# Partition shuffles with another stride and another issuing engine in a convolution-plus-MLP kernel

## The chip, the cores and the metric

The kernel runs on one core of one Trainium2 chip. Times are device microseconds (us) of one launch. The time before the change is 325.86 us, the median of two runs (324.25 and 327.46).

A core has five engines that take their instructions in order: PE (matmul), ACT (scalar engine), DVE (vector engine), POOL (GpSimd) and SP, which only issues here. Copies between memories go through 16 DMA engines. SP, ACT and POOL can each issue such transfers, on queues of their own.

## What is computed

```python
def _A_ref(q, k, v, shift_k, ssm_k, ssm_D):      # q, k, v: 1 x 2048 x 448
    k_shift = ...                                # causal convolution of k with 4 taps
    kv = k_shift * v
    y = irfft(rfft(kv, 4096) * rfft(ssm_k, 4096))[:2048]   # long convolution
    y = y + kv * ssm_D
    return q * y

def _B_ref(x, w1, b1, w2, b2):
    h = layernorm(x)
    u = gelu(einsum("bsd,sf->bdf", h, w1) + b1)  # f = 1792
    y = einsum("bdf,fs->bds", u, w2) + b2
    return y.transpose(0, 2, 1)

h  = x + _A_ref(layernorm(x), k, v, shift_k, ssm_k, ssm_D)
h2 = h + _B_ref(layernorm(h), w1, b1, w2, b2)    # x = q; layernorm over the 448 channels
```

The calls to the FFT are shortened here; the FFT runs along the sequence, each of the 448 channels on its own, and the sequence of 2048 is padded to 4096. All inputs and the output are bf16.

## The kernel before, in words

**Layout.** A sequence position is written as 16 q + r, with q on the 128 partitions and r = 0..15 along the partition. So each input is a tile of 128 x 16 x 448. All tiles lie at fixed offsets of one SBUF tensor, `arena`; PSUM is one tensor `ps` of eight banks, each 128 x 512 floats.

**The FFT as two stages of matmuls with a shuffle between.** Stage 1 (`emit_stage1`, L828) takes each r in turn: two matmuls (L832 with the cosine table `Ct`, L834 with the sine table `St`), which give 128 frequencies x 448 channels, real and imaginary, in a pair of PSUM banks; one evacuation (L839, on ACT or DVE) into one of eight ring buffers `WR`, 128 partitions x 1,792 bytes; then a *shuffle*, a DMA (L841) from that ring buffer into the tile T. The shuffle reads all 128 partitions and writes eight: source partition 16 i + j becomes row j of destination partition r + 16 i (`T[r:128:R]`, R = 16). After the 16 shuffles T holds, for row j, all 16 values of r on the partitions, and stage 2 (`emit_stage2`, L848) runs per row j four matmuls (L854) with 128 x 128 tables that mix the 16 partitions of one group, and one evacuation (L621/L622 on ACT, L624/L625 on DVE, all through the helper `evac`) in place. This is done for the filter `ssm_k` (tile TK, tag "k") and for kv (tile TU, tag "u").

**Products and inverse transform.** `emit_products_i1` (L872) multiplies the two spectra row by row (L877, L882 on DVE), runs eight matmuls per row (L888), evacuates, and sends the row through a third set of 16 shuffles (L893, `TZ[j:128:R]`) into TZ. `emit_i2` (L943) is the last stage: per r three matmuls into one bank (L951 adds kv times D, L953 and L955 use the transposed tables `CTt`, `STt` made by PE transposes in `emit_ct`, L864), then the product with the normalised q (L958), the residual (L961) and the statistics for the second layernorm (L964, L967, L971 to L983; the power -0.5 runs on POOL, L975 and L978). The first layernorm, of q, is `emit_q` (L914 to L927, its power on POOL, L919 and L922). `emit_kvd` (L935) multiplies kv by D.

**MLP.** L1017 and L1025 multiply by w1 (14 chunks of 128), L1008 is the gelu, L1034 multiplies by w2, L1037 adds, L1041 and L1044 store. The weights lie in memory that earlier tiles leave free and are loaded from ACT's queue: L996 (first part of w1, two transfers of 1,536 KB), L999 (the rest), L1004 (w2, four transfers). The first w2 transfer overwrites rows of TU that the third set of shuffles reads.

**The tables.** `emit_tables` (L630) makes `Ct` and `St` and the four block tables CC, NCC, SS, NSS (cosine and sine, with both signs) with iotas on POOL, integer and mask work on DVE (L671 to L724) and sines on ACT. The same four block tables serve stage 2 and the inverse transform.

**What sets the order.** All operations are first collected with what they read and write, then a list scheduler (`_Sched.schedule`, L236) gives each to an engine at a time of its own model and so fixes the order of every engine's instructions. It takes the ready operation with the longest remaining path first. Its costs are constants: issuing a DMA costs 450 ns on SP or ACT and 1,100 on POOL; a transfer uses `keng` DMA engines (8 for a shuffle) at 22 bytes per ns each. Buffers in rings (PSUM banks, the eight `WR`) are acquired at the moment of issue in the model: an operation that writes a pair takes any two free banks. Waits are then emitted from the true dependencies, on semaphores.

Of the kernel before, what the change touches and what calls it, by code (L numbers as in the profile page):

```python
# [71 lines left out]
class _Pool:  # L72
    def __init__(self, n):
        self.n = n
        self.free_t = [0.0] * n
        self.prev = [[] for _ in range(n)]
# [21 lines left out]
class _Sched:  # L98
# [137 lines left out]
    def schedule(self):  # L236
# [41 lines left out]
        def can_acquire(o):  # L278
            need = {}
            for b in o.acq:  # L280
                need[b.pool] = need.get(b.pool, 0) + b.k
            for p, k in need.items():
                if sum(1 for x in p.free_t if x <= t + 1e-6) < k:
# [195 lines left out]
def _build(nc, A_q, A_k, A_v, A_shift_k, A_ssm_k, A_ssm_D, B_w1, B_b1, B_w2, B_b2, out):  # L479
# [52 lines left out]
    o_SM = o_CC + 4 * 256  # L532
    SMALL = o_SM
    NSMALL = 3328

    ctx = ExitStack()
    with ctx:
# [43 lines left out]
        CC = view(o_CC, [128], f16)  # L581
        NCC = view(o_CC + 256, [128], f16)
        SS = view(o_CC + 512, [128], f16)
        NSS = view(o_CC + 768, [128], f16)
# [15 lines left out]
        psum = _Pool(8)  # L600
# [6 lines left out]
        def Ppair(b):  # L607
            s0, s1 = b.slots
            return PS[:, s0:s1 + 1:s1 - s0, 0:D]
# [4 lines left out]
        FX = ("act", "dve")  # L614

# [14 lines left out]
        def emit_tables():  # L630
# [6 lines left out]
            o_p = small(16)  # L637
# [3 lines left out]
            pc = view(o_p, [4], i32)  # L641
            pcf = view(o_p + 8, [2], f32)
# [3 lines left out]
            o_dv = o_TT + 4 * (HALF + 128)  # L646
            o_sv = o_dv + 4 * (HALF + 128)
            pi_ = view(o_pi, [HALF + 128], i32)
            dv_ = view(o_dv, [HALF + 128], f32)
            ssm = view(o_sv, [128], f32)  # L650
            csm = view(o_sv + 512, [128], f32)
            msk = view(o_sv + 1024, [128], f32)
            chi = view(o_sv + 1536, [128], i32)
            idi = view(o_sv + 2048, [128], i32)
# [9 lines left out]
            op("pool", lambda e, W: e.iota(idi, [[1, 128]], base=0, channel_multiplier=-1), w=[(o_sv + 2048, 512)],  # L664
# [5 lines left out]
               w=[(o_sv + 1536, 512)], n=128, kind="iota")  # L670
            op("dve", lambda e, W: e.tensor_single_scalar(out=ID, in_=idi, scalar=0.0, op=ALU.is_equal),  # L671
               r=[(o_sv + 2048, 512)], w=[(o_ID, 256)], n=128)
            op("dve", lambda e, W: e.tensor_copy(out=IH, in_=ID), r=[(o_ID, 256)], w=[(o_IH, 256)], n=128)
            op("dve", lambda e, W: e.tensor_scalar(out=pc[:, 1:2], in0=pc[:, 0:1], scalar1=15, scalar2=None,
                                                   op0=ALU.bitwise_and), r=[(o_p, 4)], w=[(o_p + 4, 4)], n=1)
            op("dve", lambda e, W: e.tensor_copy(out=pcf[:, 0:1], in_=pc[:, 1:2]), r=[(o_p + 4, 4)],
               w=[(o_p + 8, 4)], n=1)
            op("dve", lambda e, W: e.tensor_scalar(out=pc[:, 1:2], in0=pc[:, 0:1], scalar1=4, scalar2=None,
                                                   op0=ALU.logical_shift_right), r=[(o_p, 4)], w=[(o_p + 4, 4)], n=1)
            op("dve", lambda e, W: e.tensor_copy(out=pcf[:, 1:2], in_=pc[:, 1:2]), r=[(o_p + 4, 4)],  # L680
               w=[(o_p + 12, 4)], n=1)
            for h in range(2):
                n = HALF if h == 0 else HALF + 128
# [6 lines left out]
                if h == 1:  # L690
                    op("dve", lambda e, W: e.tensor_scalar(out=pi_[:, HALF:HALF + 128], in0=cmod,
                                                           scalar1=pcf[:, 0:1], scalar2=None, op0=ALU.mult),
                       r=[(o_cm, 512), (o_p + 8, 4)], w=[(o_pi + 4 * HALF, 512)], n=128)
# [406 lines left out]
```

## Time and profile before

The profile is one execution. "Busy" is the time in which an engine ran instructions; times in the trace count from the start of the span.

| | |
|---|---|
| median of the runs shown | 325.86 us |
| the profiled execution | 326.04 us |
| its span, first to last instruction | 324.2 us |
| busy: PE, DVE, ACT, POOL | 66%, 37%, 34%, 6% |
| mean granted clock of PE | 0.783 of full speed |
| moved by DMA | 35.95 MB, 111 GB/s over the span |
| bytes in the 48 shuffles | 48 x 224 KB = 11.0 MB |
| stages by time, us | loads and filter transposes to 23; stage 1 and shuffles 23 to 105 (stage 2 of k inside); stage 2 of u 105 to 147; products and inverse 147 to 202; last shuffle to 214; last stage and statistics to 229; MLP 229 to 324 |

How to read the rows in the next part. A row of the *chain* has its start, its length and what it was: the chain is followed back from the last instruction to whatever released it. A row of *busy time by stretch* has the stretch, its length, then for PE, PE's weight loads, DVE, ACT and POOL the busy time (and the count), then the granted PE clock, the mean busy share of the 16 DMA engines and the GB/s moved. A row of the *timeline* has start, length, engine, line, operation, what is written and read, and in brackets the idle time before it with what ended that. SPq and ACTq are the queues' issues. A row of *waits* has who waited for whom, total us, times, longest. A row of *one line's instructions* has shortest, median and longest ns, and the first and last start.

### The profile page before, as it was taken

The page shows a single profiled execution, that of the slowest core. Times are in us where ns is not written, and L with a number is a line of the kernel's source. Part 1 is how long each engine was busy: PE and PEld are TensorE (multiplying, and loading weights), DVE is VectorE, ACT ScalarE, POOL GpSimd, SP SyncE. Part 2 cuts the span into 40 slices and gives each one's busy share as a digit, 9 for nine tenths or more (in the row PEclk, how much of TensorE's full clock was granted, in tenths as well). Part 3 has the DMA queues.
Part 4 walks back from the last instruction along what each step waited for, and adds up shares of the span by engine and source line. Part 5 has one row for each costly group of instructions (what it writes and reads, how often), then busy time and mean ns, then how long its engine had stood idle before and what let it go on. Part 6 is the DMA issues. An engine that isn't in the chain of part 4 may idle for free.

```text
span 324.2 us, 2484 instructions
## 1 busy us (share of the span) xinstructions
PE 213.5 (66%) x913; PEld 96.8 (30%) x913; DVE 121.5 (37%) x241; ACT 110.0 (34%) x168; POOL 18.3 (6%) x45
## 2 busy tenths in 40 slices
PE   0656434474960766667766446065799999999994
PEld 0511000011330211112222112022354445667772
DVE  8499980006670597001244400049730000003034
ACT  6597434453440333332233223026970122210000
POOL 1000000001020024000000000000530000000000
PEclk9978555559795665555599959559599999999999
DMA  7996555555996000001229579629500000000022
GB/s 199 294 433 176 108 108 111 110 110 114 163 204 175 14 0 0 0 0 27 53 66 259 140 232 271 171 49 381 232 1 0 2 0 0 2 0 28 30 85 86
DMA packets 16279, 35.95 MB, mean 111 GB/s; under 512 B 1100, under 2 KB 10572, under 8 KB 16139
## 3 DMA queue, kind: packets, MB, share of 16 engines
q1 hardware_dynamic: 10250, 21.11, 25.3%
q10 hardware_dynamic: 6016, 14.68, 16.0%
q8 instruction: 7, 0.11, 0.1%
q14 instruction: 6, 0.04, 0.1%
HBM read 22.94 MB, written 1.84 MB: 76 GB/s over the span
## 4 chain that ended last, share of the span: by engine, by line
PE 47%; DMA 31%; ACT 13%; DVE 5%; issue 1%; SPq 1%; DVEq 0%; ACTq 0%
DMA arena<-arena 28%; PE ps L1034 13%; ACT arena L621 10%; PE ps L888 10%; PE ps L854 8%; PE ps L1025 8%; PE ps L1017 6%; DMA arena<-in_A_ssm_k_dram 3%; ACT arena L839 3%; DVE arena L958 2%; DVE arena L961 1%; PE ps L817 1%; DVE arena L1037 1%; SPq L743 0%; DVE arena L624 0%
## 5 line engine op out<-in xcount | busy, mean ns | idle before, releaser
L854 PE MATMUL ps<-arena 128*128 128x448 bf16 x128 | 43.0, 491 | 31.1 <-ACT arena L621 13.6
L621 ACT CAST arena<-ps 128x896 bf16<-128x896 f32 (+1 forms) x32 | 28.2, 881 | 78.7 <-PE ps L854 38.0
L888 PE MATMUL ps<-arena 128*128 128x448 bf16 x128 | 34.4, 424 | 20.8 <-ACT arena L621 20.8
L1034 PE MATMUL ps<-arena 128*128 128x448 bf16 x224 | 45.6, 355 | 0.0
L1037 DVE SCALAR_TENSOR_TENSOR arena<-ps,arena 128x448 bf16<-128x448 f32 x16 | 9.7, 677 | 69.0 <-PE ps L1034 69.0
L839 ACT CAST arena<-ps 128x896 bf16<-128x896 f32 x29 | 25.6, 931 | 29.4 <-DMA arena<-arena 26.2
L1034 PEld LDWEIGHTS ps<-arena 128*128 128x128 bf16 x224 | 31.5, 145 | 13.5 <-ACT arena L1008 3.1
L832 PE MATMUL ps<-arena 128*128 128x448 bf16 x32 | 16.0, 501 | 25.7 <-ACT arena L839 19.9
L854 PEld LDWEIGHTS ps<-arena 128*128 128x128 f16 x128 | 13.2, 119 | 59.8 <-ACT arena L621 23.8
L1025 PE MATMUL ps<-arena 128*128 128x448 bf16 x128 | 29.4, 353 | 0.0
L1017 PE MATMUL ps<-arena 128*128 128x448 bf16 x96 | 23.7, 386 | 5.8 <-DVE arena L983 5.8
L877 DVE TENSOR_TENSOR arena<-arena 128x896 bf16<-128x896 bf16 x16 | 10.0, 625 | 43.5 <-PE ps L888 42.6
L888 PEld LDWEIGHTS ps<-arena 128*128 128x128 f16 x128 | 12.9, 111 | 42.6 <-ACT arena L621 29.9
L1008 ACT ACTIVATE arena<-ps,arena 128x448 bf16<-128x448 f32 x14 | 8.9, 633 | 40.4 <-PE ps L1017 21.1
L958 DVE TENSOR_TENSOR arena<-ps,arena 128x448 bf16<-128x448 f32 x16 | 9.4, 623 | 29.7 <-PE ps L955 29.6
L798 DVE TENSOR_TENSOR arena<-arena 128x1792 bf16<-128x1792 bf16 x16 | 16.5, 1098 | 4.0 <-DMA arena<-in_A_k_dram 4.0
L832 PEld LDWEIGHTS ps<-arena 128*128 128x128 f16 x32 | 3.3, 102 | 46.7 <-ACT arena L839 38.5
L834 PE MATMUL ps<-arena 128*128 128x448 bf16 x32 | 16.5, 516 | 0.0
L1025 PEld LDWEIGHTS ps<-arena 128*128 128x128 bf16 x128 | 12.0, 98 | 12.6 <-ACT arena L1008 2.4
L964 ACT ACTIVATE arena<-arena 128x448 bf16<-128x448 bf16 x16 | 9.2, 576 | 17.3 <-PE ps L953 16.9
L1017 PEld LDWEIGHTS ps<-arena 128*128 128x128 bf16 x96 | 10.1, 106 | 16.3 <-DVE arena L983 6.3
L953 PE MATMUL ps<-arena 128*128 128x448 bf16 x16 | 6.8, 425 | 11.2 <-DMA arena<-arena 11.2
(74 smaller groups left out, 184.4 us busy)
## 6 DMA issues: line engine op xcount, KB each, us to landing
arena<-arena SPq DMA_DIRECT2D x48, 224.0 KB
arena<-in_B_w_dram ACTq DMA_DIRECT2D x5, 2048.0 KB, 9.9
arena<-in_B_w_dram ACTq DMA_DIRECT2D x2, 1536.0 KB, 25.6
arena<-in_A_ssm_k_dram SPq DMA_DIRECT2D x4, 448.0 KB, 7.8
arena<-in_A_k_dram SPq DMA_DIRECT2D x4, 448.0 KB, 12.4
arena<-in_A_v_dram SPq DMA_DIRECT2D x4, 448.0 KB, 13.0
arena<-in_A_q_dram SPq DMA_DIRECT2D x1, 1792.0 KB, 19.0
out_dram<-arena SPq DMA_DIRECT2D x7, 224.0 KB, 1.9
```

The costliest lines, as they stand in the source:

```text
L621: return e.copy(out=dst(), in_=src())
L798: op("dve", lambda e, W, T=T, i=i, r=r: e.tensor_tensor(out=T[:, i], in0=KH[:, r:r + 4, :], in1=WT, op=ALU.mult), r=[(o_KH + r * DB, 4 * D ...
L832: op("pe", lambda e, W, b=b, r=r: e.matmul(Pb(b, 0), Ct[:, r, :], src[:, r, :], start=True, stop=True), r=[r_C(r), (o_src + r * DB, DB)], ...
L834: op("pe", lambda e, W, b=b, r=r: e.matmul(Pb(b, 1), St[:, r, :], src[:, r, :], start=True, stop=True), r=[r_S(r), (o_src + r * DB, DB)], ...
L839: return e.copy(out=dst, in_=Ppair(b)) if W == "act" else e.tensor_copy(out=dst, in_=Ppair(b))
L854: op("pe", lambda e, W, b=b, bi=bi, tab=tab, ci=ci, st=st, sp=sp, j=j: e.matmul(Pb(b, bi), tab, T[:, j, ci, :], start=st, stop=sp), r=rr, ...
L888: i = op("pe", lambda e, W, b=b, bi=bi, tab=tab, mi=mi, m=m, k=k: e.matmul(Pb(b, bi), tab, MR(m.slots[0])[:, mi, :], start=(k % 4 == 0), s ...
L958: op("dve", lambda e, W, b=b, r=r: e.tensor_tensor(out=V[:, r, :], in0=Pb(b), in1=Q[:, r, :], op=ALU.mult), r=[(o_Q + r * DB, DB)], w=[(o_ ...
L1017: op("pe", lambda e, W, r=r, fc=fc, b=bs[fc]: e.matmul(Pb(b), W1A[:, r, 128 * fc:128 * fc + 128], Q[:, r, :], start=(r == 0), stop=(r == R ...
L1025: op("pe", lambda e, W, r=r, fc=fc, b=b: e.matmul(Pb(b), W1B[:, r, 128 * (fc - n0):128 * (fc - n0) + 128], Q[:, r, :], start=(r == 0), sto ...
L1034: op("pe", lambda e, W, r=r, fc=fc, b=b: e.matmul(Pb(b), W2[:, fc, r:S:R], G[:, fc, :], start=(fc == 0), stop=(fc == NFC - 1)), r=[(o_W2 + ...
L1037: op("dve", lambda e, W, r=r, b=b: e.scalar_tensor_tensor(out=X[:, r, :], in0=Pb(b), scalar=b2c[:, r:r + 1], in1=X[:, r, :], op0=ALU.add, ...
```

## The change

**Stride and issuer.** Shuffle r now writes the eight partitions p0, p0 + 4, ..., p0 + 28 with p0 = 32 (r >> 2) + (r & 3), in place of r, r + 16, ..., r + 112. All three sets of shuffles are issued from POOL (`SHQ`), where descriptors are written by software, in place of SP.

**What follows from it.** Partition 32 a + 4 i + b now holds frequency group i and value r = 4 a + b. Stage 2 therefore gets block tables of its own (FC, FS, FNS) beside the four that the inverse transform keeps, so there are seven. For the last stage, the tables are reordered before they are transposed: four copies of 128 x 1,024 elements on POOL (`emit_ct`).

**PSUM pairs.** A pair of banks is now an aligned pair (0 and 1, 2 and 3, ...), and a single bank is taken by preference where the other half of its pair is in use. The evacuation reads two adjacent banks.

```diff
 class _Pool:
-    def __init__(self, n):
+    def __init__(self, n, pairs=False):
...
+        def pick(p, k):
+
+            ok = [x <= t + 1e-6 for x in p.free_t]
+            if k == 1:
+                best = None
+                for i in range(p.n):
+                    if ok[i]:
+                        key = (p.pairs and ok[i ^ 1], p.free_t[i], i)
+                        if best is None or key < best:
+                            best = key
+                return None if best is None else [best[2]]
+            best = None
+            for i in range(0, p.n, 2):
+                if ok[i] and ok[i + 1]:
+                    key = (max(p.free_t[i], p.free_t[i + 1]), i)
+                    if best is None or key < best:
+                        best = key
+            return None if best is None else [best[1], best[1] + 1]
...
-                        fr = sorted((x, i) for i, x in enumerate(p.free_t) if x <= t + 1e-6)[:b.k]
-                        b.slots = sorted(i for _, i in fr)
+                        b.slots = pick(p, b.k)
...
-        psum = _Pool(8)
+        psum = _Pool(8, pairs=True)
...
+        SHQ = ("pool", "pool")
...
-                n = HALF if h == 0 else HALF + 128
+                n = HALF if h == 0 else HALF + 256
...
+            for k, (so, sgn, i) in enumerate(((1, 1.0, 0), (0, 1.0, 0), (0, -1.0, 0), (1, 1.0, 1), (1, -1.0, 1),
+                                              (0, 1.0, 1), (0, -1.0, 1))):
+                src = (ssm, csm)[so][:, 128 * i:128 * i + 128]
+                op("dve", lambda e, W, k=k, src=src, sgn=sgn, i=i: e.scalar_tensor_tensor(
+                    out=BD[k], in0=src, scalar=sgn, in1=msk[:, 128 * i:128 * i + 128], op0=ALU.mult, op1=ALU.mult),
...
-                op("sp", lambda e, W, w=w, r=r: e.dma_start(T[r:128:R].rearrange("p j c d -> p j (c d)"),
-                                                            WR(w.slots[0]).rearrange("p c d -> p (c d)")),
+                p0 = 32 * (r >> 2) + (r & 3)
+                op(SHQ[r % 2], lambda e, W, w=w, p0=p0: e.dma_start(
+                    T[p0:p0 + 29:4].rearrange("p j c d -> p j (c d)"),
+                    WR(w.slots[0]).rearrange("p c d -> p (c d)")),
...
-                for bi, tab, ci, st, sp in ((0, CC, 0, True, False), (0, NSS, 1, False, True),
-                                            (1, SS, 0, True, False), (1, CC, 1, False, True)):
+                for bi, tab, ci, st, sp in ((0, FC, 0, True, False), (0, FNS, 1, False, True),
+                                            (1, FS, 0, True, False), (1, FC, 1, False, True)):
...
         def emit_ct():
...
+                    op("pool", lambda e, W, cp=cp, tab=tab, h=h: e.tensor_copy(
+                        out=cp.rearrange("p r (h f l) -> p r h f l", h=4, f=8),
+                        in_=tab[:, 8 * h:8 * h + 8, :].rearrange("p r (f h l) -> p r h f l", f=8, h=4)),
+                       r=[(o_tab + 2048 * h, 2048)], w=[(oc, 2048)], n=1024)
...
-                op("sp", lambda e, W, j=j: e.dma_start(TZ[j:128:R].rearrange("p r c d -> p r (c d)"),
-                                                       TU[:, j].rearrange("p c d -> p (c d)")),
+                p0 = 32 * (j >> 2) + (j & 3)
+                op(SHQ[j % 2], lambda e, W, j=j, p0=p0: e.dma_start(
+                    TZ[p0:p0 + 29:4].rearrange("p r c d -> p r (c d)"), TU[:, j].rearrange("p c d -> p (c d)")),
```

More of the change, by code (lines that the diff above doesn't have):

```diff
@@ L72 @@
 class _Pool:
-    def __init__(self, n):
+    def __init__(self, n, pairs=False):
         self.n = n
+        self.pairs = pairs
         self.free_t = [0.0] * n
@@ L282, in can_acquire @@
             for p, k in need.items():
-                if sum(1 for x in p.free_t if x <= t + 1e-6) < k:
+                if pick(p, k) is None:
                     return False
             return True
+        def pick(p, k):
[15 more added lines that the diff above has]
+            return None if best is None else [best[1], best[1] + 1]
         while done < n:
@@ L580, in _build @@
         IH = view(o_IH, [128], f16)
[L581 to L584, printed above, removed]
+        BD = [view(o_CC + 256 * k, [128], f16) for k in range(7)]
+        FC, FS, FNS, CC, NCC, SS, NSS = BD
         def WR(s):
@@ L640, in emit_tables @@
             srow = view(o_s, [16], i32)
[L641 to L642 removed]
+            pc = view(o_p, [6], i32)
+            pcf = view(o_p + 24, [4], f32)
             o_b = small(16)
@@ L645, in emit_tables @@
             o_pi = o_TT
[L646 to L654, printed above, removed]
+            o_dv = o_TT + 4 * (HALF + 256)
+            o_sv = o_dv + 4 * (HALF + 256)
+            pi_ = view(o_pi, [HALF + 256], i32)
+            dv_ = view(o_dv, [HALF + 256], f32)
+            ssm = view(o_sv, [256], f32)
+            csm = view(o_sv + 1024, [256], f32)
+            msk = view(o_sv + 2048, [256], f32)
+            chi = view(o_sv + 3072, [128], i32)
+            idi = view(o_sv + 3584, [128], i32)
             sch.boost = 3e6
```

92 lines of the change are left out of this document (51 added, 41 removed).

## The prediction

> **What bounds the kernel now.** I read the page first (span, DMA rows, chain), then the chain in order of time, then busy time by stretch, then the timeline where the chain changes hands.
>
> ```profile
> span 324.2 us, 2484 instructions
> DMA  7996555555996000001229579629500000000022
> GB/s 199 294 433 176 108 108 111 110 110 114 163 204 175 14 0 0 0 0 27 53 66 259 140 232 271 171 49 381 232 1 0 2 0 0 2 0 28 30 85 86
> PE 47%; DMA 31%; ACT 13%; DVE 5%; issue 1%; SPq 1%; DVEq 0%; ACTq 0%
> arena<-arena SPq DMA_DIRECT2D x48, 224.0 KB
> arena<-in_B_w_dram ACTq DMA_DIRECT2D x2, 1536.0 KB, 25.6
> ```
> ```profile
> 29.54 13.60 DMA arena<-arena
> ...
> 44.09 16.71 DMA arena<-arena
> ...
> 63.75 15.73 DMA arena<-arena
> ...
> 81.13 23.70 DMA arena<-arena
> 104.91 1.67 PE ps L854 x4
> ...
> 179.52 8.83 DMA arena<-arena
> ...
> 201.93 11.76 DMA arena<-arena
> ```
> ```profile
> 33.00:57.00 24.00, 10.22 (x22) 1.45 (x22) 14.04 (x18) 9.81 (x12) 0.00 (x0) 0.50 0.54 109
> 81.00:105.00 24.00, 12.92 (x79) 6.47 (x78) 12.08 (x22) 7.00 (x8) 2.88 (x5) 0.78 0.94 181
> ```
>
> The chain is the 48 shuffles' (arena to arena, 224 KB) for 31% of the span. From 33 to 57 us nothing but shuffles moves, at 109 GB/s with 0.54 of the 16 DMA engines busy (the last two columns; the page's slices of 8.1 us stay at 108 to 114 up to 81 us), and no compute engine is full. So about eight DMA engines are occupied and each moves 110/8.6 = 13 GB/s, where the slice from 16 to 24 us, which loads from DRAM, shows 433 GB/s, 27 per engine. The shuffles' engines are held up by something in the pattern, not by lack of work. One shuffle of 229,376 bytes takes 229,376/110,000 = 2.09 us.
>
> ```profile
> L841 SPq DMA_DIRECT2D arena<-arena x32: 597/597/1402, 24.0 to 81.1; - x32
> 45.87 1.18 DVE L807 TENSOR_TENSOR arena<-arena 128x896 bf16<-128x896 bf16 x2
> 79.57 1.05 ACTq L996 DMA_DIRECT2D arena<-in_B_w_dram  x2
> ```
>
> The 32 shuffles of stage 1 are issued from 24.0 to 81.1 us. The data for the last of them exist early: DVE ends the convolution (L807) at 47.05. The queue still holds shuffles when the first weights (L996, two transfers of 1,536 KB, 3.1 MB) join at 79.57, and stage 2 of u starts only at 104.91, when the last has landed. Behind that, the chain is PE and ACT in turn, with two more DMA waits (8.83 and 11.76 us) at the inverse transform's shuffles.
>
> **The change part by part.** The sum is made against the span of 324.2; the profiled execution took 326.04, so 1.84 us lie outside it, and the median of the runs shown, 325.86, is 0.2 below.
>
> *Transfer.* Each shuffle still moves the same bytes into eight partitions. Steps of four change which eight. The old rate is a row; the new one is not in the trace. Lower bound of its time: eight engines at the 27 GB/s of the DRAM slice, 216 GB/s, 1.06 us. Upper bound: the step is not what holds the engines up, 2.09 us as now. I take 1.06: the same engines move twice as much when a transfer writes all 128 partitions, and the spread of partitions written is what sets the shuffles apart. [...]
>
> *Issue.*
>
> ```profile
> L922 POOL TENSOR_TENSOR arena<-arena x8: 705/706/717, 80.7 to 127.1; 128x2 f32<-128x2 f32 x8
> L798 DVE TENSOR_TENSOR arena<-arena x16: 1089/1098/1106, 13.9 to 41.8; 128x1792 bf16<-128x1792 bf16 x16
> 80.16 0.50 POOL L919 TENSOR_SCALAR arena<-arena 128x2 f32<-128x2 f32 x1 [78.20 <-DVE arena L916]
> ```
>
> No DMA is issued by GpSimd in the trace. Lower bound: SP's 0.60 us. Upper: a POOL operation (0.71) that first sits out one DVE instruction (1.10), 1.81. I take the middle, 1.2. The issues leave SP, where only loads and output stores remain. They join POOL's in-order queue, where each waits for its evacuation; behind them stand L919/L922 (they feed L927's Q, first used at L958 after 213 us) and L975/L978 (after the last shuffle), so nobody near waits. [...]
>
> *Stage 1 to stage 2 of u.* Issue (1.2) is now slower than transfer (1.06), so the 32 shuffles take 24.0 + 32 x 1.2 = 62.4.
>
> ```profile
> out_dram<-arena SPq DMA_DIRECT2D x7, 224.0 KB, 1.9
> L839 ACT CAST arena<-ps 128x896 bf16<-128x896 f32 x29 | 25.6, 931 | 29.4 <-DMA arena<-arena 26.2 <-PE ps L834 3.1
> 117.37 1.68 PE L854 MATMUL ps<-arena 128*128 128x448 bf16 x4 [1.00 <-ACT arena L621]
> ```
>
> Landing adds 1.9 (an output store of the same size): 64.3. The W1 load is tied to the end of stage 1's reads and comes earlier too; all of its 3.1 MB ahead of the last shuffle cost 7.3 us at 433 GB/s, none cost 0; I take 4: 68.3. What is late next: V is ready at 47.05; 32 evacuations at 0.93 end near 53; the 16 groups of stage 2 of k (0.93 each by their evacuations, 1.68 if their matmuls stay as slow as in the row at 117) start near 45, when k has landed, and end between 60 and 72. So 68.3 stands, 104.9 - 68.3 = **36.6 us** gained. With both bounds of the issue: 60 (then the transfer is the limit) to 91, a gain of 45 to 14; with the transfer unchanged, none.
>
> *Inverse transform.*
>
> ```profile
> ACT arena L621 <- DMA arena<-arena: 6.6, 1, 6.6
> 188.37 0.37 ACTq L1004 DMA_DIRECT2D arena<-in_B_w_dram  x1
> 190.00:202.00 12.00, 8.01 (x33) 3.06 (x32) 0.00 (x0) 3.62 (x4) 0.00 (x0) 0.85 1.01 301
> 202.00:214.00 12.00, 0.77 (x3) 0.20 (x4) 0.00 (x0) 0.00 (x0) 0.00 (x0) 0.58 0.53 136
> ```
>
> ACT stands 6.6 us because its next instruction, a W2 load (L1004) into rows that earlier shuffles still read, waits for them, and the evacuation behind it waits along. A new shuffle every 2.67 us against 1.2 leaves no backlog: **6 us** gained (0 to 8.8). After the last evacuation at 201.9 the last shuffle lands at 213.7; new: issue 1.2, landing 1.9, some 3.5 behind weights (the 301 GB/s before it), 6.6: **5 us** gained (0 to 8.7).
>
> *Small parts.* Three more half tables and a second mask: some ten short DVE operations, 2 us.
>
> ```profile
> 13.93 1.09 DVE L798 TENSOR_TENSOR arena<-arena 128x1792 bf16<-128x1792 bf16 x1 [4.02 <-DMA arena<-in_A_k_dram]
> 14.94 0.49 DVE L722 SCALAR_TENSOR_TENSOR arena<-arena 128x128 f16<-128x128 f32 x2
> ```
>
> They fall in DVE's 4.02 us wait for k; one pair of tables is made inside the convolution. I charge 1 us (0 to 2, all of it if the cover is gone). [...] PSUM pairs must now be adjacent banks: same bytes per evacuation, 0 by itself.
>
> Sum: +1 - 36.6 - 6 - 5 = -46.6; 324.2 - 46.6 + 1.84 = 279.4, less the 0.2 to the median: **279 us**. Its own range: 264 to 300.
>
> **The rivals.**
>
> ```profile
> 93.07 0.92 PE L951 MATMUL ps<-arena 128*128 128x448 bf16 x4
> 109.03 0.95 PE L951 MATMUL ps<-arena 128*128 128x448 bf16 x2
> PE ps L854 <- ACT arena L621: 13.6, 14, 1.0
> PE ps L888 <- ACT arena L621: 20.8, 16, 5.8
> 24.00:33.00 9.00, 5.77 (x19) 1.08 (x18) 9.00 (x12) 7.09 (x9) 0.00 (x0) 0.87 0.67 178
> ```
>
> A: *banks come free too.* Six L951 matmuls run early and each holds a PSUM bank until i2, so stage 2 of u and the inverse transform go through one pair of banks: matmuls, then 1.00 us for the evacuation; PE's waits for it come to 13.6 + 20.8, of which 5.8 are the DMA stall counted above: 28.6. Another order of the planner (POOL is costed at 1,100 for a DMA, SP at 450) could leave a second pair and save them: **251 us**. For it: the wait is in nearly every group. Against: singles still take what is free when PE idles.
>
> B: *DVE locks POOL out.* If POOL writes no descriptors while DVE runs, nothing is issued until 47.05 (DVE is busy 9.00 of 9.00 us from 24): 47.05 + 38.4 + 1.9 + 4 = 91.4, a gain of 13.5 instead of 36.6: **302 us**. For it: 706 ns for two elements shows POOL's start-up is long, but not why. [...]
>
> C: *the rate stays.* The engines are held up by their reads or by the 1,792-byte pieces: 2.09 us stay, one table microsecond and a longer issue twice are added: **328 us**. Against it: the 433 GB/s slice; for it: no row shows a step of four.
>
> D: *slower.* Descriptors written in software cost more per shuffle than the transfer did. Place: POOL's queue from 24 us. It decides from (104.9 - 24 - 1.9 - 4)/32 = 2.34 us per shuffle on, 2.7 when the other 11 us are kept. At 3.0: 24 + 96 + 5.9 = 125.9, +21; the inverse transform's shuffles, one per 2.67, fall behind too and eat the rest: **347 us**. Against: 1.81 is the longest that rows make likely.
>
> **How the numbers follow.** Forecast 0.57, A 0.15, B 0.13, C 0.08, D 0.07. The range 250 to 310 holds nearly all of the forecast (0.55), half of A and most of B (0.12), some 0.75 to 0.8. Two per cent, 6.5 us, is about what a measurement of this kernel tells from no change: faster is forecast, A and B, 0.85; within, C, 0.08; slower, D, 0.07.
>
> **What would show it.** Right: between 33 and 60 us the DMA rows near 200 GB/s; shuffles from POOL about 1.2 us apart; L854 for u starting near 68; no 6.6 us wait of ACT; i2 within 7 us of the last evacuation; 95 us of MLP unchanged. Wrong: 110 GB/s still (C), no shuffle before 47 (B), shuffles over 2.3 us apart with DMA engines idle (D), stage 2 of u without its 1.00 us gaps (A).

## The result, and the profile after

The changed kernel takes **249.31 us** (median of two runs, 249.02 to 249.59) against 325.86 before: a ratio of 0.765, 95% interval 0.748 to 0.782. That lies just below the range of 250 to 310 and 30 us below the forecast of 279. It is within 2 us of what rival A gave (251), in part by luck, as the table below shows. Ratios here and below leave out runs that are over 1.5% above the fastest of the same kernel; medians and ranges are of all runs.

First the page of the changed kernel: the slices of 6.2 us, the queue on which the shuffles now go, the chain's shares, and the row of the shuffles' issues (line 873 is line 841 of before).

```profile
span 247.8 us, 2495 instructions
PEclk9996775559997999999987599899999999999998
DMA  5999799999970001489999299100000000001023
GB/s 185 282 369 434 215 201 203 192 241 253 240 217 7 0 0 30 122 222 268 233 366 322 65 352 405 79 1 0 3 0 0 0 0 3 0 33 43 2 109 111
q0 software_dynamic: 5376, 11.04, 19.5%
PE 53%; DMA 21%; DVE 11%; ACT 6%; POOL 3%; issue 3%; SPq 1%; DVEq 0%; ACTq 0%; POOLq 0%
arena<-arena POOLq DMA_DIRECT2D x48, 224.0 KB, 8.3
L873 POOL DMA_DIRECT2D arena<-arena x32 | 19.5, 608 | 25.6 <-ACT arena L870 19.8
```

Where 108 to 114 GB/s stood for six slices of 8.1 us (33 to 81 us), 192 to 253 stand in eight slices of 6.2 us now (25 to 74 us), the last input loads and part of the weights among them. DMA's share of the chain is 21% instead of 31%. One issue on GpSimd takes 608 ns in the mean; a shuffle lands 8.3 us after its issue (median).

The chain of the changed kernel in order of time, where it changes hands:

```profile
30.72 9.97 DMA arena<-arena
...
41.91 7.61 DMA arena<-arena
...
66.04 8.31 DMA arena<-arena
...
74.44 2.48 PE ps L887 x8
```

Stage 2 of u starts at 74.44 instead of 104.91. Its 16 rows and the inverse transform are the surprise. Busy time by stretch, first of before for these two stages, then of after, where the first four rows are the shuffles of k and u (the first with the last input loads in it, the third and fourth with w1) and the last two are the same two stages:

```profile
105.00:146.80 41.80, 26.73 (x70) 7.40 (x70) 18.16 (x47) 14.49 (x16) 6.11 (x10) 0.54 0.01 4
146.80:202.00 55.20, 34.42 (x129) 12.95 (x130) 13.96 (x24) 14.48 (x16) 0.00 (x0) 0.79 0.56 151
```
```profile
24.00:33.00 9.00, 6.60 (x21) 1.21 (x20) 9.00 (x12) 8.10 (x11) 6.20 (x10) 0.81 0.82 224
33.00:42.00 9.00, 5.02 (x13) 0.89 (x14) 9.00 (x12) 5.56 (x8) 3.67 (x7) 0.57 1.04 205
42.00:60.00 18.00, 13.54 (x40) 3.70 (x38) 10.03 (x18) 12.56 (x15) 8.17 (x14) 0.65 0.95 223
60.00:74.40 14.40, 10.60 (x61) 5.00 (x61) 13.41 (x31) 7.81 (x9) 7.19 (x12) 1.00 0.93 232
74.40:92.00 17.60, 17.19 (x87) 7.60 (x87) 13.50 (x22) 10.99 (x12) 0.00 (x0) 0.90 0.01 2
92.00:129.00 37.00, 27.15 (x130) 12.23 (x130) 21.22 (x45) 13.02 (x16) 12.17 (x20) 0.95 0.74 200
```

Stage 2 of u moves nothing by DMA in either kernel (4 and 2 GB/s), so no faster shuffle can help it, and yet it fell from 41.9 to 17.6 us. PE is busy for 17.19 of 17.60 us at a granted clock of 0.90; before it was busy for 26.7 of the 41.8 us of the row, at 0.54. The stages, to the nearest tenth:

| stage, us | before | after | forecast |
|---|---|---|---|
| stage 2 of u starts at | 104.9 | 74.4 (-30.5) | 68.3 (-36.6) |
| stage 2 of u | 41.9 | 17.6 (-24.3) | 0 |
| products and inverse, to the last evacuation | 55.1 | 36.8 (-18.3) | -6 |
| last evacuation to the last stage | 11.8 | 9.5 (-2.3) | -5 |
| last stage and statistics | 15.5 | 15.5 | 0 |
| MLP | 95.0 | 93.8 (-1.1) | 0 |
| table work | | 0 | +1 |

Of 76.4 us in all, 42.6 come from the two stages for which the forecast had 6. Rival A priced these two at 34.6 (28.6 and the 6) and all the rest at 40.6, where 33.9 was measured: two misses of 8 and 7 us that cancel.

The timeline of the changed kernel, at the places that matter below:

```profile
58.88 1.07 DVE L870 CAST arena<-ps 128x896 bf16<-128x896 f32 x1
...
64.00 1.07 DVE L870 CAST arena<-ps 128x896 bf16<-128x896 f32 x1
...
65.37 1.28 POOL L873 DMA_DIRECT2D arena<-arena  x2 [1.43 <-DVE arena L870]
...
82.82 0.35 PE L991 MATMUL ps<-arena 128*128 128x448 bf16 x1
...
83.05 0.93 PE L887 MATMUL ps<-arena 128*128 128x448 bf16 x4
...
122.61 0.91 ACT L639 CAST arena<-ps 128x896 bf16<-128x896 f32 x1 [5.68 <-DMA arena<-arena]
...
138.43 0.56 PE L993 MATMUL ps<-arena 128*128 128x448 bf16 x1 [8.56 <-DMA arena<-arena]
```

Two of u's last evacuations (L870) sit on DVE between other work and end at 59.95 and 65.07, and ACT's last one, behind stage 2 of k, runs from 64.54 to 65.44; so the last two shuffles are issued only from 65.37 on. Only four identity matmuls (L991, L951 of before) run ahead of the inverse transform, one at a time from 82.82 to 85.93, where six did before. The four matmuls of a row of stage 2 take 0.93 us instead of 1.68, with no wait in front. ACT's stall in front of a w2 load is still there: 5.68 us.

### The profile page after: what moved, and what is told of

The parts are those of the page before. It is cut to its first block, busy times and chain, and to the rows that moved or that the text cites. A ratio compares the mean times of both kernels' runs of the same rounds, so it can differ in the third digit from the quotient of the medians.

```text
span 247.8 us, 2495 instructions
## 1 busy us (share of the span) xinstructions
PE 190.3 (77%) x913; PEld 95.2 (38%) x913; DVE 130.1 (53%) x253; ACT 105.4 (43%) x164; POOL 51.6 (21%) x97
## 4 chain that ended last, share of the span: by engine, by line
PE 53%; DMA 21%; DVE 11%; ACT 6%; POOL 3%; issue 3%; SPq 1%; DVEq 0%; ACTq 0%; POOLq 0%
DMA arena<-arena 18%; PE ps L1074 17%; PE ps L1065 10%; PE ps L1057 8%; PE ps L887 7%; PE ps L927 7%; ACT arena L639 5%; DMA arena<-in_A_ssm_k_dram 4%; DVE arena L998 3%; POOL arena L873 2%; PE ps L848 2%; DVE arena L1001 2%; DVE arena L954 1%; DVE arena L1077 1%; ACT arena L870 1%
## 5 line engine op out<-in xcount | busy, mean ns | idle before, releaser
L1074 PE MATMUL ps<-arena 128*128 128x448 bf16 x224 | 45.6, 355 | 0.0
L887 PE MATMUL ps<-arena 128*128 128x448 bf16 x128 | 31.2, 386 | 6.8 <-DMA arena<-arena 2.9
L639 ACT CAST arena<-ps 128x896 bf16<-128x896 f32 (+1 forms) x24 | 20.4, 876 | 33.1 <-PE ps L927 18.1
L927 PE MATMUL ps<-arena 128*128 128x448 bf16 x128 | 27.0, 366 | 9.0 <-ACT arena L639 9.0
L1065 PE MATMUL ps<-arena 128*128 128x448 bf16 x128 | 29.4, 353 | 0.0
L870 ACT CAST arena<-ps 128x896 bf16<-128x896 f32 x30 | 25.5, 940 | 6.3 <-DMA arena<-arena 6.3
L1057 PE MATMUL ps<-arena 128*128 128x448 bf16 x96 | 22.6, 372 | 5.2 <-DVE arena L1023 5.2
L873 POOL DMA_DIRECT2D arena<-arena x32 | 19.5, 608 | 25.6 <-ACT arena L870 19.8
L863 PE MATMUL ps<-arena 128*128 128x448 bf16 x32 | 15.1, 471 | 12.3 <-ACT arena L870 7.8
L927 PEld LDWEIGHTS ps<-arena 128*128 128x128 f16 x128 | 12.2, 101 | 23.9 <-ACT arena L639 12.9
L887 PEld LDWEIGHTS ps<-arena 128*128 128x128 f16 x128 | 11.7, 105 | 23.7 <-issue 6.2
L642 DVE CAST arena<-ps 128x896 bf16<-128x896 f32 x9 | 9.6, 1089 | 14.7 <-PE ps L927 9.6
L865 PE MATMUL ps<-arena 128*128 128x448 bf16 x32 | 15.5, 485 | 0.0
L863 PEld LDWEIGHTS ps<-arena 128*128 128x128 f16 x32 | 3.3, 102 | 30.2 <-ACT arena L870 22.9
```

Of the source, the lines that this page charges most:

```text
L639: return e.copy(out=dst(), in_=src())
L863: op("pe", lambda e, W, b=b, r=r: e.matmul(Pb(b, 0), Ct[:, r, :], src[:, r, :], start=True, stop=True), r=[r_C(r), (o_src + r * DB, DB)], ...
L865: op("pe", lambda e, W, b=b, r=r: e.matmul(Pb(b, 1), St[:, r, :], src[:, r, :], start=True, stop=True), r=[r_S(r), (o_src + r * DB, DB)], ...
L870: return e.copy(out=dst, in_=Ppair(b)) if W == "act" else e.tensor_copy(out=dst, in_=Ppair(b))
L873: op(SHQ[r % 2], lambda e, W, w=w, p0=p0: e.dma_start(T[p0:p0 + 29:4].rearrange("p j c d -> p j (c d)"), WR(w.slots[0]).rearrange("p c d - ...
L887: op("pe", lambda e, W, b=b, bi=bi, tab=tab, ci=ci, st=st, sp=sp, j=j: e.matmul(Pb(b, bi), tab, T[:, j, ci, :], start=st, stop=sp), r=rr, ...
```

## The experiments

Each batch ran beside the kernel before on its own chip: medians of 321.8, 322.1, 320.2 and 321.6 us. The changed kernel itself was not run again beside them, so a time here is set against its 249.3 us only across chips. The theory to be tested: two things were gained, the rate of the shuffles (by the partitions that they write) and a second pair of PSUM banks (by the order that the planner chose); the issuer gains nothing by itself.

### Stride or issuer

The changed kernel in its own order, but with its shuffles issued by SP:

```diff
+            if o.is_dma and o.eng == "pool":
+                o.eng = "sp"
             W = o.eng
```

> The changed kernel with its order of instructions kept, but every shuffle issued by SP instead of POOL; the stride stays four. Theory P (the eight partitions written set the rate): shuffles still move at about 200 GB/s, now with about half of the 16 DMA engines busy, stage 2 of u starts near 74 us, time 247 to 253 us. Theory E (the issuer sets the rate, because it keeps 16 engines in work instead of eight): the rate falls back to 110 GB/s, stage 2 of u starts near 105 us, the inverse transform's shuffles lag by some 6 us, time about 285 us.

Measured: 251.9 us (250.7 to 253.1), ratio 0.781 (0.774 to 0.788). And the reverse, GpSimd as the issuer and the old step:

```diff
-                p0 = 32 * (r >> 2) + (r & 3)
+                p0 = r
...
-                    T[p0:p0 + 29:4].rearrange("p j c d -> p j (c d)"),
+                    T[p0:128:R].rearrange("p j c d -> p j (c d)"),
...
-                for bi, tab, ci, st, sp in ((0, FC, 0, True, False), (0, FNS, 1, False, True),
-                                            (1, FS, 0, True, False), (1, FC, 1, False, True)):
+                for bi, tab, ci, st, sp in ((0, CC, 0, True, False), (0, NSS, 1, False, True),
+                                            (1, SS, 0, True, False), (1, CC, 1, False, True)):
...
```

> The changed kernel with the old stride of sixteen (and the tables that belong to it), still issued by POOL, same order of instructions. Theory P: 110 GB/s again, whatever the share of busy engines, stage 2 of u near 105 us, time about 285 us. Theory E: about 200 GB/s as in the changed kernel, time 247 to 253 us.

Measured: 283.3 us (282.6 to 286.8), ratio 0.880 (0.872 to 0.889). Busy time by stretch between 33 us and the end of the shuffles of k, first with SP and steps of four, then with GpSimd and steps of sixteen; the last two columns are the share of the 16 DMA engines and GB/s:

```profile
33.00:42.00 9.00, 5.83 (x16) 0.95 (x16) 9.00 (x12) 7.00 (x8) 0.00 (x0) 0.74 0.53 199
```
```profile
33.00:57.00 24.00, 11.13 (x24) 1.56 (x24) 14.22 (x18) 11.20 (x13) 7.14 (x12) 0.50 1.05 120
```

The rate goes with the step far more than with the issuer: 199 GB/s from half of the engines, 120 from all of them. GpSimd as issuer is worth 2.6 us by the medians, if anything, at steps of four; at steps of sixteen it moves 120 GB/s where SP moved 109, and stage 2 of u starts at 96.9 instead of 104.9 (the expectation was 110 GB/s and 105 us). With the old step the kernel is still 38.5 us faster than before, and only 8 of these lie in that start: the rest needs another cause.

### Aligned pairs, or the order

The kernel before with the change's allotment of banks alone (its choice of the free pair comes along and is left out here):

```diff
-        psum = _Pool(8)
+        psum = _Pool(8, pairs=True)
```

> The kernel before with nothing changed but the allocation of PSUM banks: aligned pairs, singles packed beside singles. In the order that results, four L951 matmuls instead of six come before stage 2 of u, so two pairs of banks stay for stage 2 of u and the inverse transform. Theory A (a missing pair of banks cost the 42 us that these two stages lost): shuffles as before, stage 2 of u still near 105 us, then stage 2 of u and inverse together 55 to 70 us instead of 97, time 284 to 300 us. Rival (those stages got faster because faster shuffles keep PE at the full clock): 322 to 327 us, no change.

Measured: 322.1 us (318.5 to 324.9), ratio 1.001 (0.996 to 1.006). No change; and what I had assumed, four early identity matmuls, did not come about: the order still has six (four together and two more), so one pair is left. Next, the same with the identity matmuls held until the inverse transform has ended, so that all four pairs are free:

```diff
-                       r=[(o_ID, 256), (o_V + r * DB, DB)], bw=[b], n=D)
+                       r=[(o_ID, 256), (o_V + r * DB, DB)], bw=[b], n=D, safter=i1_last[-1:])
```

> As the run with the allocation alone, and besides no L951 matmul may come before the last matmul of the inverse transform, so all four pairs of banks stay free. Theory A: a little faster than with two pairs where the evacuation's wait is left (0.8 us per two rows, some 6 us), 278 to 296 us. Rival (two pairs suffice, or the clock decides): the same as the allocation alone.

Measured: 299.1 us (295.6 to 300.1), ratio 0.923 (0.914 to 0.933). Stage 2 of u falls to 15 us (104.6 to 119.7), as the theory of the banks has it, but of those 27 us some are handed back: the chain of this kernel ends up in shuffles again.

```profile
81.26 23.30 DMA arena<-arena
...
104.61 4.74 PE ps L873 x17
...
146.10 13.83 DMA arena<-arena
...
163.22 21.20 DMA arena<-arena
```

The rows of the inverse transform now come faster than they are carried off at the old step: the last shuffle lands 21.2 us after its issue (13.8 us more go to an earlier wait), with weights beside it. So a good part of the second pair's gain needs the faster shuffles. The time is just above what was expected (278 to 296).

Then the planner alone. The kernel before, SP issuing, steps of sixteen, banks as before; one constant of the model is changed, so that a shuffle's issue counts 1,100 ns, as it does for GpSimd:

```diff
-            o.est = {e: (450.0 if e != "pool" else 1100.0) for e in o.engs}
+            o.est = {e: (450.0 if e != "pool" and keng != 8 else 1100.0) for e in o.engs}
```

> The kernel before with one constant of the planner changed: it costs the issue of a shuffle at 1,100 ns, as it does for GpSimd, instead of 450; SP still issues, the stride stays sixteen, banks are allotted as before. In the order that comes out, no identity matmul stands before the end of stage 2 of u and six stand in the inverse transform after its row 5 (two pairs or more until then, one after). Order theory (the second pair came from the planner's cost alone): stage 2 of u starts near 104 and takes 15 to 18 us instead of 42; the inverse transform is then held by one pair and by shuffles at 110 GB/s, 45 to 55 us; 322 - 25 = 297 us, 290 to 305. Rival (the allotment of aligned pairs or the faster shuffles are needed for it): 320 to 324 us.

Measured: 296.5 us (296.2 to 296.9), ratio 0.927 (0.922 to 0.931). Busy time by stretch of this kernel, stage 2 of u and the inverse transform:

```profile
105.70:121.50 15.80, 14.51 (x66) 6.40 (x67) 12.48 (x18) 7.67 (x9) 0.00 (x0) 0.90 0.00 1
121.50:173.00 51.50, 33.63 (x152) 13.79 (x150) 21.02 (x46) 16.08 (x19) 4.01 (x6) 0.84 0.67 162
```

Not one transfer is different, and stage 2 of u takes 15.8 us instead of 41.8. The order of the planner did it: no identity matmul comes before 129.4 us, six of them then leave one pair for the rest of the inverse transform. The control is the changed kernel with the old allotment of any two free banks:

```diff
-        psum = _Pool(8, pairs=True)
+        psum = _Pool(8)
...
-            return PS[:, s0:s1 + 1, 0:D]
+            return PS[:, s0:s1 + 1:s1 - s0, 0:D]
```

> The changed kernel with the old allotment of PSUM banks: a pair is any two free banks, and a single takes the bank that is free longest. Its order still has four identity matmuls early. Order theory: four banks stay for pairs, any two of them make one, so two pairs as in the changed kernel: 249 us, 246 to 252. Rival (aligned pairs are what leaves the second pair): stage 2 of u near 40 us again, 275 to 290 us.

Measured: 247.7 us (246.6 to 252.8), ratio 0.773 (0.768 to 0.778). Aligned pairs cost and bring nothing; the order with four early identity matmuls is what counts.

### One pair put back into the changed kernel

Stage 2 of u and the inverse transform may use banks 6 and 7 alone, the identity matmuls the other six; step, issuer and all else as changed:

```diff
+        LIMU, LIMS = (6, 8), (0, 6)
...
-                b = _Buf(psum, 2)
+                b = _Buf(psum, 2, LIMU if T is TU else (0, 8))
...
-                b = _Buf(psum, 2)
+                b = _Buf(psum, 2, LIMU)
...
-                    b = _Buf(psum)
+                    b = _Buf(psum, 1, LIMS)
```

> The changed kernel (stride of four, GpSimd) with one thing put back: stage 2 of u and the inverse transform may use only one pair of PSUM banks, and the identity matmuls that add kv times D take the other six, six of them early, as in the kernel before. Banks theory (the 42 us that stage 2 of u and the inverse transform lost came from a second pair of banks): stage 2 of u starts at 74 as in the changed kernel, then takes about 40 us instead of 17.6 with a wait of 1.0 us in front of each group and a granted clock near 0.55, the inverse transform 45 to 55 instead of 37; 249 + 22 + 12 = 283 us, 275 to 292. Rival (these stages shortened because the shuffles got faster, whatever the banks): stage 2 of u 18 us, inverse 37, 249 to 253 us.

Measured: **280.0 us**, the median of 274.9, 279.4, 280.7 and 283.0. The spread is wide, and the profile is of the run with 280.7. Busy time by stretch of stage 2 of u, the inverse transform and the wait for its last shuffle, then a row of the timeline (line 891 is 854 of before):

```profile
73.20:111.90 38.70, 25.44 (x79) 8.01 (x77) 13.50 (x33) 15.42 (x17) 3.71 (x6) 0.59 0.00 0
112.90:160.40 47.50, 31.44 (x128) 12.24 (x128) 13.93 (x24) 14.57 (x17) 9.03 (x15) 0.88 0.55 159
160.40:168.30 7.90, 0.22 (x2) 0.14 (x3) 0.00 (x0) 0.17 (x1) 0.60 (x1) 0.61 0.96 309
```
```profile
88.98 1.68 PE L891 MATMUL ps<-arena 128*128 128x448 bf16 x4 [1.00 <-ACT arena L643]
```

The groups of before are back: 1.68 us of matmuls, 1.00 us of wait, clock 0.59. So in the changed kernel the second pair is worth 280.0 - 247.7 = 32.3 us (against the any-two-banks run of the same batch, which has the changed kernel's order), or 27.6 from the lowest run (274.9 against 247.3, the median of the three lower runs there). And without it the change gains 320.2 - 280.0 = 40.2 us, 45.3 by the lowest run, where the forecast, which left this pair out, had 46.6.

### More banks still

The changed kernel with the identity matmuls held, as above, so that all four pairs are free:

> The changed kernel, but no L991 matmul (kv times D, L951 before) is placed ahead of the last inverse matmul, so all four pairs of banks stay free. Theory A (what is left of the pair shortage, 0.8 us per two rows of the inverse transform): 242 to 246 us. Rival (the shuffles and the weights that travel with them set the end of the inverse transform): 247 to 250 us, the gain turns up as a longer wait for DMA before i2.

Measured: 249.3 us (248.9 to 250.0), ratio 0.779 (0.774 to 0.784): as the changed kernel. Stage 2 of u ends earlier (88.8, with 92.1 in the changed kernel) and the matmuls of the inverse transform too (124.0, with 128.1), but ACT's stall is 6.87 us and the last stage starts at 137.9 instead of 138.4. Behind the second pair, shuffles and weights set the end.

### The weights

The first part of w1, which the changed kernel issues from ACT at 47.35 beside u's shuffles, goes out on SP behind the last of these; then the same with the rest of w1 and w2 behind the last shuffle of the inverse transform as well:

```diff
-        for oid in order:
+        for oid in seq:
             o = self.ops[oid]
+            if oid in self.late:
+                o.eng = "sp"
+                o.extra = list(o.extra) + self.sh[self.late[oid]]
             W = o.eng
...
```

> The changed kernel with its order kept, but the first w1 load (two transfers of 1,536 KB) is issued by SP once the last shuffle of u has landed. Theory W (the load travelled with the shuffles at about 225 GB/s together and delayed the last shuffle of u): stage 2 of u starts near 67 us instead of 74, time 239 to 245 us. Rival (the last u shuffles are late because their evacuations are, at 59 and 64 us): start within 3 us of 74, time 246 to 250 us.

Measured: 246.9 us (246.6 to 247.8), ratio 0.771 (0.766 to 0.776). Stage 2 of u starts some 2 us earlier, at 72.5. In this kernel's timeline, the last shuffle of u, the w1 load that waits for its landing, and the start of stage 2 of u:

```profile
66.63 0.60 POOL L893 DMA_DIRECT2D arena<-arena  x1 [0.90 <-ACT arena L889]
...
70.21 1.02 SPq L1058 DMA_DIRECT2D arena<-in_B_w_dram  x2
...
72.49 1.69 PE L907 MATMUL ps<-arena 128*128 128x448 bf16 x8
```

The evacuations still hold the last issue up to 66.6, but the shuffle now lands 3.6 us after it and not 8.3. So w1 did cost 4 to 5 us of landing; only 2 are gained, because PE is at stage 2 of k until 71.5 and waits for its last evacuation until 72.45.

> As the run with the first w1 load held back, and the rest of w1 and all of w2 are issued by SP too, once the last shuffle of the inverse transform has landed. Theory W: ACT no longer stands 5.7 us in front of a w2 load, and the last shuffle lands some 4 us after its evacuation instead of 9.5: 11 us less, 228 to 236 us. Rival (the weights then come too late for the MLP): PE waits for weights, 240 us or more.

Measured: **236.8 us** (235.5 to 237.6), ratio 0.738 (0.731 to 0.744), just above the expected 228 to 236. Rows of this kernel's chain, and its busy time in the inverse transform and in the wait behind it:

```profile
87.56 3.08 PE ps L947 x15
...
120.50 4.57 DMA arena<-arena
```
```profile
87.50:118.50 31.00, 25.34 (x128) 11.69 (x128) 20.37 (x44) 12.09 (x14) 12.16 (x20) 1.00 0.38 95
118.80:125.10 6.30, 1.00 (x5) 0.23 (x4) 1.09 (x1) 0.82 (x1) 1.18 (x2) 0.80 0.39 107
```

ACT's stall is gone, the inverse transform takes 32.1 us at full clock (87.6 to 119.6), the last shuffle lands 5.5 us after the last evacuation instead of 9.5, and the MLP, although the rest of w1 is issued at 125.1 instead of 105.5 and 117.5, still takes 95 us. So what was left of the DMA wait in the changed kernel was weights ahead of shuffles. Both edits together:

> As the run with all weights held back, and with all four pairs of banks free in the inverse transform. If the terms add: 222 to 232 us, faster than each alone. If shuffles, one per 1.06 us at the least, or PE at 1.6 us a row set the pace: the same as without the banks, 228 to 236 us.

Measured: 243.4 us (239.7 to 244.8), ratio 0.753 (0.742 to 0.765): slower than the late weights alone. Neither expectation was met, and the two don't add. With all pairs free the planner runs the inverse transform four rows at a time, and PE then waits for the products that DVE makes of the next four:

```profile
87.23 6.25 PE L947 MATMUL ps<-arena 128*128 128x448 bf16 x32
95.78 6.23 PE L947 MATMUL ps<-arena 128*128 128x448 bf16 x32 [2.29 <-DVE arena L941]
...
114.50 7.91 PE L947 MATMUL ps<-arena 128*128 128x448 bf16 x32 [2.29 <-DVE arena L941]
```

The waits add up to little more than with late weights alone (three of 2.29 us against seven of 0.81). What is lost is in the last two groups, which take 7.91 us instead of 6.25, and behind them, where the last shuffle lands 6.3 us after its issue instead of 4.6.

### The other half of the partitions

What in the written partitions sets the rate? Shuffles 0 to 7 write below partition 64, 8 to 15 above. This version lets them alternate (0, 8, 1, 9, ...) for k and in the inverse transform; the rows of stage 2 follow the same order (the last change below stands twice):

```diff
+        ALT = [8 * (i & 1) + (i >> 1) for i in range(R)]
...
-            for r in range(R):
+            for r in (ALT if tag == "k" else range(R)):
...
-            for j in range(R):
+            for j in ALT:
```

> The changed kernel with another order of the shuffles only: those of k and those of the inverse transform go in the order 0, 8, 1, 9, 2, 10, ... so that one writes below partition 64 and the next above; those of u keep their order. Theory of the written partitions (the eight partitions of one shuffle, or the set of rows they belong to, limit the rate, and two shuffles in flight on different halves don't share that limit): between 24 and 42 us, where k's shuffles go, over 240 GB/s, up to the 283 that one issue of 229,376 bytes per 0.81 us allows, instead of 224 and 205; the time is 246 to 250 us, as those of u and DVE set the end. Rival (what limits the rate lies in the engines, the pieces of 1,792 bytes or the reads, and has nothing to do with the half): 200 to 225 GB/s there, 249 us.

Measured: 239.6 us (238.0 to 242.1), ratio 0.746 (0.739 to 0.753).

```profile
24.00:33.00 9.00, 7.01 (x22) 1.21 (x20) 9.00 (x12) 8.46 (x11) 6.48 (x11) 1.00 0.79 216
33.00:42.00 9.00, 6.30 (x17) 1.14 (x18) 9.00 (x12) 6.94 (x10) 4.98 (x9) 0.62 0.82 233
```

The rate is 216 and 233 GB/s, not over 240, though the engines are busy for 0.79 and 0.82 of the time instead of 0.82 and 1.04. The stretch that tells most is 36.4 to 42.7 us, in which no weights move yet, this version's evacuations wait for nothing, and GpSimd issues a shuffle every 0.81 us, enough for 283 GB/s. The changed kernel first, then this one:

```profile
36.40:42.70 6.30, 4.50 (x11) 0.79 (x12) 6.30 (x9) 4.19 (x5) 2.99 (x5) 0.50 1.04 202
36.40:42.70 6.30, 5.94 (x17) 0.98 (x16) 6.30 (x9) 6.30 (x9) 4.75 (x8) 0.61 0.74 215
```

So 215 GB/s moved where 283 were on offer: issuing was not what held the shuffles, and two halves in flight do not add up; they gain 6%. That is nearer to the rival than to the theory. What limits the rate at steps of four stays open, and so does why the busy share falls to 0.74 at that rate.

The 10 us that this version gains were not foreseen. By the profiles 2.0 lie ahead of the inverse transform, 4.7 in it (90.0 to 122.1, no ACT stall, 32.1 us as with late weights) and 1.8 in the wait for its last shuffle. With the new row order the planner sends the rest of w1 at 114.9 and 115.4 instead of 105.5 and 117.5, and w2 from 128.3 on, after the inverse transform, instead of from 122.2. So it is mostly the weights again, moved by chance.

> The same order of shuffles in the fastest version so far (first part of w1 after the last shuffle of u, the other weights after the last shuffle of the inverse transform, 236.8 us). There the shuffles of the inverse transform come slower than they can be moved (95 GB/s in that stretch), so both theories expect no gain from it: 235 to 238 us; only the rate between 24 and 42 us tells them apart, over 240 GB/s or 200 to 225.

Measured: 234.7 us (233.2 to 235.6), ratio 0.731 (0.724 to 0.738). With the weights out of the way the alternating order gains nothing that can be told apart (236.8 in another batch, and the intervals of the ratios overlap), as both theories had it. The rate between 33 and 47 us, where only shuffles move in both, first with late weights alone, then with the alternating order as well:

```profile
33.00:47.00 14.00, 8.88 (x20) 1.29 (x21) 14.00 (x19) 9.50 (x12) 5.96 (x10) 0.53 1.03 201
33.00:47.00 14.00, 9.77 (x26) 1.65 (x26) 14.00 (x18) 10.13 (x14) 7.84 (x14) 0.63 0.81 217
```

Again 217 GB/s from 0.81 of the engines, 8% above the order of before, and in the rival's 200 to 225. The time is the lowest measured here.

## Why the prediction was wrong, step by step

**The step that failed** is the sum itself: "+1 - 36.6 - 6 - 5" has no term for the 97 us from 105 to 202 but ACT's stall. The second pair of banks stood in rival A ("Another order of the planner (POOL is costed at 1,100 for a DMA, SP at 450) could leave a second pair"), priced at 28.6 us, with a chance of 0.15. Measured: 27.6 to 32.3 us. The argument held against it, "singles still take what is free when PE idles", came true for four identity matmuls and not for six, and four leave the second pair. That pairs are "0 by itself" was right (322.1 and 247.7). What decides is how many identity matmuls the planner puts ahead of the inverse transform, and its constant for the issue changes with the issuer: six early with 450 in the kernel before, four with 1,100 in the changed kernel, none ahead of the end of stage 2 of u with 1,100 in the kernel before (296.5 us). The changed kernel planned with 450 was not run, so that it would have had six again is not shown. A change of the issuer in this kernel is a change of the schedule, and the sum took the schedule as given.

**With the pair put back the forecast's own case holds:** 274.9 to 283.0 us, with 320.2 before on that chip, against 279 with 325.86 before: ratios of 0.859 to 0.884 and 0.856. Its terms, one by one:

*Transfer, 1.06 us a shuffle.* Nearly right: from 33 us on, where only shuffles move, 199 to 205 GB/s, which is 1.15 to 1.12 us. That eight engines would reach the 27 GB/s each of the DRAM slice was an estimate; with SP issuing, 0.53 of the 16 were busy and moved 199/8.5 = 23 each. Steps of four moved 199 GB/s from SP and 205 from GpSimd, steps of sixteen 109 from SP and 120 from GpSimd; why the rate goes with the step is not shown. Two shuffles on different halves did not add up (215 against 202, 217 against 201).

*Issue, 1.2 us.* Half of that: 0.608 us, 0.81 from start to start while DVE is busy 9.00 of 9.00 us, so rival B is out as well. Rival C falls with 199 to 205 GB/s, rival D with 0.81 us per shuffle. "So nobody near waits" was not quite so: the powers of the first layernorm stand between the shuffles on GpSimd, and two shuffles whose evacuations end by 56.4 are issued only from 57.94 on, behind one (L959) that had waited for DVE.

*Stage 1 to stage 2 of u, 36.6.* 30.5 measured, 32.5 with one pair (72.4). The start was missed by 6 us, because the pace was not that of the issue. From 30.7 to 49.5 us the chain goes through landings (9.97 and 7.61 us): an evacuation waits there for a ring buffer that a shuffle still reads. From there to 65.37 it goes through stage 2 of k on PE and other work on DVE, so "32 evacuations at 0.93 end near 53" took for free what was not: they end at 65.07 on DVE and at 65.44 on ACT. Then comes a landing of 8.3 us where 1.9 plus 4 were taken. With w1 away the landing is 3.6 us, and then stage 2 of k, which was to "end between 60 and 72", holds PE until 72.5.

*Inverse transform, 6.* 0.9 in the changed kernel, where the stall is 5.68 instead of 6.61. With one pair put back ACT waits for no shuffle there, and the stage is 55.1 - 47.3 = 7.8 us shorter: "a new shuffle every 2.67 us" against the new rate leaves no backlog, as predicted. In the changed kernel the rows come faster (31 us for 16 without the stall, 1.9 each) while the rest of w1 travels along, and the stall is back. One gain took away the cover of another. (With w1 and w2 both moved the stall is gone; w1 was not moved alone there.)

*Last shuffle, 5.* 2.3 measured, 3.9 with one pair, 6.3 with the weights late.

*Tables, +1.* 0: the first product of the convolution starts at 13.76 us instead of 13.93.

## What to carry to other kernels

Where a list scheduler plans with constants, a change of an engine or a cost is also a change of order: compare the orders of the two programs before you take any stage for unchanged, and give the stages that the change doesn't touch a term of their own. A wait that stands in front of nearly every group of a stage (matmuls 1.68, wait 1.00) is worth its full price and the lost clock (0.59 here, 0.90 without the wait), so look at who holds the buffers. And when shuffles become fast, look next at what shares their engines: moving the weights behind them gave another 12 us here (249.3 to 236.8, on different chips; ratios of 0.765 and 0.738).

## What was not expected of the hardware

**A busy share of 1.0 is not a rate.** On SP's queue a shuffle keeps half of the 16 engines busy, on GpSimd's all of them, at about the same bytes: 0.53 and 199 GB/s against 1.04 and 205. With steps of sixteen it is 0.54 and 109 against 1.05 and 120. A full row of the page's DMA digits would have looked like the limit of the engines; with the source read in the same way, it went with the partitions that are written.

**Weights beside shuffles.** From 42 to 74 us shuffles and w1 together move 223 to 232 GB/s, hardly more than the 205 of shuffles alone, although loads alone reach 434. They take from each other: in the changed kernel the last shuffle of u lands 8.3 us after its issue, and 3.6 us with w1 moved away. With SP as the issuer of the shuffles the first 18 us move more:

```profile
42.00:60.00 18.00, 12.47 (x35) 2.84 (x34) 9.73 (x16) 10.26 (x13) 1.22 (x2) 0.69 0.77 278
```

So 223 is not a limit of the two kinds of transfer together; it goes with the issuer too. Why is not shown.

**Half the clock and the full clock, beside the same gaps.** The chain of the changed kernel with one pair, at the border from groups of four to groups of eight matmuls, each group with 1.00 us of wait in front:

```profile
110.37 1.69 PE ps L891 x4
113.05 3.18 PE ps L931 x8
...
125.55 1.70 PE ps L931 x8
```

Four matmuls in 1.69 us (busy for 63% of the time) went on at a clock of 0.59 for 38 us. After 12 us of eight in 3.18 (76%) the clock came up, and from then on eight took 1.70, again 63%, at full speed. The kernel before does the same: eight in 3.18 from 146.78 to 162.46 at a granted clock of 0.50, then eight in 1.70 at 1.00 (163.44 to 182). Over stage 2 of u the clock was 0.59 with one pair and 0.90 with two, and yet at the same 63% of busy time it stayed at 0.59 for 38 us in one stage and at full speed for over 30 in the next. What grants it is not shown.
